# Agent attention with a maxout network: constant matmuls and the order of work at the end of the first stage

## Chip, core and metric

The kernel runs on one core of a Trainium2 chip. The metric is device time in microseconds (us) for one launch. Before the change the median of 5 runs is 474.26 us (473.52 to 474.63). The profile is one more execution of the same program.

## What is computed

The inputs have 4 batches of 12544 tokens with 128 channels, and 49 agents per batch. Attention goes from the agents to the tokens, then from the tokens to the agents, and a maxout network with three first layers follows:

```python
scale = 1.0 / np.sqrt(q.shape[-1])
def sm(a, b):
    s = scale * (a @ b.transpose(0, 2, 1))
    e = np.exp(s - s.max(-1, keepdims=True))
    return e / (e.sum(-1, keepdims=True) + 1e-09)
agent_v = sm(agents, k) @ v          # 4 x 49 x 128
x = (sm(q, agents) @ agent_v).reshape(B * S, D)
h = np.maximum(np.maximum(x @ w1, x @ w2), x @ w3)   # 768 wide
out = h @ w_out
```

For each batch, agent_v can be multiplied with the weights once. The kernel does so: "the product" of a batch is a table G of 49 rows that holds agent_v times the weights (and times differences of weights), and a query's exponentials are then multiplied with G directly.

## The kernel before

**First stage.** The product of batch 0 needs all keys and values of batch 0. They come in 12 groups, ten of 9 blocks of 128 tokens and two of 4 blocks (groups 10 and 11). One group goes through these steps (`k_group` with `early` set):

- SP issues the loads of keys and values (L218) into a pool of 14 buffers, `st`.
- GpSimd (POOL in the profile) casts the keys (L223), ScalarE (ACT) casts the values (L228).
- TensorE (PE) turns the keys, block by block, into PSUM (`turn_k`, L237), and VectorE (DVE) copies them out (`evacuate`, L243).
- TensorE computes the scores (L255), ACT the exponentials (L260).
- TensorE multiplies the exponentials with the values (L266) and with ones for their sums (L269), DVE adds both to an accumulator (L276).

These steps are staggered: the scores of a group stand behind the turning of the next group, its values behind the turning of the one after that.

**End of the first stage.** `k_tail` takes the reciprocal of the sums (L335) and multiplies (L338) into `avT`. `product` then runs ten matmuls in two halves (L350); ACT copies the first half out to G (L357), DVE the second (L355). Query group 0 is turned by TensorE (`turn_q`, L413), copied by DVE (L417), scored (L427), and ACT takes its exponentials (L433).

**Second stage.** There are 49 query groups. Each goes through hidden matmuls against G (L453), relu and maximum on ACT and DVE (L468, L465, L476, L478) and output matmuls (L483, L492). The first query groups also "host" one key group each of the next batch. Host key group 0 is turned on TensorE (L237). Later ones are turned by a DMA that SP issues (L239), so their scores (L255) wait for that DMA. GpSimd casts their keys (L223) and values (L230) and the queries (L408). In the first query groups there is no output work yet, and `ramp` puts constant matmuls (L575) where it would be.

**Constant matmuls.** `keep_busy` (L200) multiplies the identity with a constant tile of 128 x 512 into a PSUM tile that nobody reads. From group 4 on, the kernel places three of them after each group's turning and three after its scores and values; more stand among the steps of the end of the first stage.

**Order.** Every step is put into a list by `at(key, ...)`, with a key that is its place in time on an invented scale (6.0 units for a group), the names it needs, and the PSUM ring that it takes a tile from. `emit` sorts the list and issues the steps in that order, a step that lacks what it needs being put off until it can go. There are two rings: `uv`, three tiles of two banks, and `om`, two tiles of one bank. Each engine executes its own instructions in the order of issue. The tile framework adds the semaphore waits. `last_key` is the key of group 11, two units ahead of `KEY["u0"]`, the first hidden matmuls of query group 0.

Of the kernel before, what the change touches and what calls it, by code (L numbers as in the profile page):

```python
# [16 lines left out]
def kernel(  # L17
# [64 lines left out]
    def uv_tile(dtype=FP32):  # L82
        return psum.tile([P, 2, 512 if dtype == FP32 else 1024], dtype, tag="uv", bufs=3, name="uv_ps")
# [6 lines left out]
    def at(key, fn, name=None, needs=(), ring=None, frees=()):  # L90

        ops.append((key, len(ops), fn, name, needs, ring, frees))
# [55 lines left out]
    def load_tile():  # L150
        return loads.tile([P, KT, C], FP32, tag="st", name="st")
# [58 lines left out]
    def k_group(b, t0, n, key, s):  # L210

        d = {}
        early = s is None

        def load():
            for name, src in (("k", k), ("v", v)):
                t = d[name] = load_tile()
                nc.sync.dma_start(t[:, :n, :], src[b, t0 * P:(t0 + n) * P, :].rearrange(  # L218
                    "(p j) c -> p j c", j=n))

        def cast_k():
            d["kb"] = work.tile([P, KT, C], BF16, tag="k_bf", bufs=3, name="k_bf")
            nc.gpsimd.tensor_copy(out=d["kb"][:, :n, :], in_=d["k"][:, :n, :])  # L223

        def cast_v():
            d["vb"] = work.tile([P, KT, C], BF16, tag="v_bf", bufs=4, name="v_bf")
            if early:
                nc.scalar.activation(d["vb"][:, :n, :], d["v"][:, :n, :], AF.Copy)  # L228
            else:
                nc.gpsimd.tensor_copy(out=d["vb"][:, :n, :], in_=d["v"][:, :n, :])  # L230

        def turn_k():
            d["kT"] = work.tile([P, KT, P], BF16, tag="kT", bufs=3, name="kT")
            if early or s == 0:
                t = d["kT_ps"] = uv_tile(BF16).rearrange("p i c -> p (i c)")
                for j in range(n):
                    nc.tensor.transpose(t[:, j * P:(j + 1) * P], d["kb"][:, j, :], ident)  # L237
            else:
                nc.sync.dma_start_transpose(out=d["kT"][:, :n, :],  # L239
                                            in_=d["kb"][:, :n, :].rearrange("p j c -> p (j c)"))  # L240

        def evacuate():
            nc.vector.tensor_copy(out=d["kT"][:, :n, :].rearrange("p j c -> p (j c)"),  # L243
                                  in_=d["kT_ps"][:, :n * P])

        def scores():
            if early:
                d["pair"] = uv_tile()
                d["s"] = d["pair"][:, 0, :]
                last_tile["t"] = d["s"]  # L250
            else:
                d["s"] = host[s]
            t = d["s"]
            for j in range(n):
                nc.tensor.matmul(t[:, j * A:(j + 1) * A], d["kT"][:, j, :], agT[:, b, :A],  # L255
                                 start=(j == 0), stop=True, skip_group_check=True)

        def exps():
            d["e"] = work.tile([P, KT * A], BF16, tag="e_k", bufs=3, name="e_k")
            nc.scalar.activation(d["e"][:, :n * A], d["s"][:, :n * A], AF.Exp, scale=scale)  # L260

        def values():
            t, c = (d["pair"][:, 1, :], 0) if early else (d["s"], CV)
            for j in range(n):
                e = d["e"][:, j * A:(j + 1) * A]
                nc.tensor.matmul(t[:, c:c + A], d["vb"][:, j, :], e, start=(early and j == 0),  # L266
                                 stop=True, skip_group_check=True)
                if early:
                    nc.tensor.matmul(t[:, A:2 * A], ones_bf, e, start=False, stop=True,  # L269
                                     skip_group_check=True)  # L270

        def add_values():
            w = 2 * A if early else A
            src = d["pair"][:, 1, :w] if early else d["s"][:, CV:CV + A]
            if t0:
                nc.vector.tensor_tensor(out=Vacc[b], in0=src, in1=Vacc[b], op=ALU.add)  # L276
            else:
                Vacc[b] = work.tile([P, w], FP32, tag=f"Vacc{w}", name="Vacc")
                nc.vector.tensor_copy(out=Vacc[b], in_=src)

        def add_exps():
            if t0:
                nc.gpsimd.tensor_tensor(out=Eacc[b][:, :n * A], in0=Eacc[b][:, :n * A],  # L283
                                        in1=d["e"][:, :n * A], op=ALU.add)
            else:
                Eacc[b] = work.tile([P, KT * A], FP32, tag="Eacc", name="Eacc")
                nc.gpsimd.tensor_copy(out=Eacc[b], in_=d["e"])

        if early:
            g = ("early", t0)  # L290
            at(key - 30, load)
            at(key - 5, cast_k)
            at(key - 4, cast_v)
            at(key, turn_k, ("kt", g), (), "uv", [("kt_out", g)])
            at(key + 0.5, evacuate, ("kt_out", g), [("kt", g)])

            last = [("normalise", 0)] if t0 + n == NT else []
            at(min(key + 6.6, last_key + 0.6), scores, ("ks", g), [("kt_out", g)], "uv",
               [("ka", g)] + last)
            at(min(key + 7, last_key + 0.65), exps, ("ke", g), [("ks", g)])  # L300
            done = last_key + (0.55 if key < last_key - 6.5 else 0.8)
            at(min(key + 13.2, done), values, ("kv", g), [("ke", g)])
            at(min(key + 13.6, done + 0.01), add_values, ("ka", g), [("kv", g)])
        else:
            at(key + KEY["ks"] - 22, load)
            at(max(key + KEY["ks"] - 10, last_key - 3.4), cast_k)
            at(max(key + KEY["ks"] - 8, last_key - 3.3), cast_v)
            if s:
                at(max(key + KEY["ks"] - 6.5, last_key - 3.2), turn_k, ("kt_out", s))
            else:  # L310
                at(last_key + 0.87, turn_k, ("kt", s), (), "uv", [("kt_out", s)])
                at(last_key + 1.6, evacuate, ("kt_out", s), [("kt", s)])
            at(key + KEY["ks"], scores, ("ks", s), [("kt_out", s), ("ho", s)])
            at(key + KEY["ke"], exps, ("ke", s), [("ks", s)])
            at(key + KEY["ke"] + 1.5, add_exps, ("kx", s), [("ke", s)])
            at(key + KEY["kv"], values, ("kv", s), [("ke", s)])
            at(key + KEY["ka"], add_values, ("ka", s), [("kv", s)])
# [63 lines left out]
    def q_group(s):  # L381
        pairs = [range(0, 2), range(2, 4)]
        n, nh = GT, GT // 2
        parts = split(s * GT, (s + 1) * GT, 2)
        key = 6.0 * s
# [125 lines left out]
        def put(name, fn, *needs, ring=None, frees=()):  # L511
            at(key + K[name], fn, (name, s), needs, ring, frees)
# [3 lines left out]
        if s == 0:  # L516
            at(last_key - 29.9, load)
            at(last_key - 3.5, cast)
            at(last_key + 0.81, turn_q, ("qt", 0), (), "om", [("qe", 0)])
            at(last_key + 0.82, evacuate, ("qe", 0), [("qt", 0)])  # L520
            at(last_key + 1.2, scores, ("s", 0), [("qe", 0)], "om", [("ex", 0)])
            at(last_key + 1.21, exps, ("ex", 0), [("s", 0)])
        elif s < SB:
            at(key + K["qt"] - 20, load)
            at(max(key + K["qt"] - 7, last_key - 3), cast)
            put("qt", turn_q, ring="om", frees=[("qe", s)])
            put("qe", evacuate, ("qt", s), *([("s", s - 3)] if s >= 3 else []))
        else:
            at(key + K["s"] - 24, load)
            at(key + K["s"] - 8, cast)  # L530
            at(key + K["s"] - 5.5, turn_q_dma, ("qe", s))
# [47 lines left out]
    first_sizes = [KT] * (NT // KT) + ([NT % KT // 2, NT % KT - NT % KT // 2] if NT % KT else [])  # L579
    last_key = KEY["u0"] - 2  # L580
# [7 lines left out]
    fillers = []  # L588
    for g, n in enumerate(first_sizes):
        k_group(0, sum(first_sizes[:g]), n, first_key + 6.0 * g, None)  # L590

        if g >= 4:
            fillers += [(first_key + 6.0 * g + 0.55, 3), (first_key + 6.0 * g + 1.3, 3)]
    k_tail(0, last_key, (KEY["u0"] - 0.15, KEY["u0"] - 0.14), None)
    for key, n in fillers + [(last_key + 0.88, 3), (KEY["u0"] - 0.05, 4)]:
        at(key, lambda n=n: keep_busy(n), ("busy", key), (), "om", [("busy", key)])
    tails = {b * NT // GT: b for b in range(1, B)}
    hosting = set()
    for b in range(1, B):
        for g in range(NK):  # L600
            s = (b - 1) * NT // GT + g
# [5 lines left out]
    for s in range(NQ):  # L607
        q_group(s)
# [34 lines left out]
```

## Time and profile before

| what | us |
| --- | --- |
| median of 5 runs | 474.26 |
| lowest, highest | 473.52, 474.63 |
| profiled execution | 473.19 |
| its span, first to last instruction | 471.3 |
| TensorE busy in the span | 441.2 (94%) |
| DVE, ACT, POOL busy | 407.9, 395.8, 166.3 |
| turning of group 9 starts | 39.52 |
| last value matmul of the first stage starts | 46.69 |
| product starts | 49.49 |
| scores of host key group 0 start | 51.24 |

Times of events are us from the start of the span. The chain of work that ended last is found from the last instruction backwards: at each step to what released it, or to the instruction before it on its engine. In the timeline a row has the start, the duration, the engine, the line, the operation and its tiles; in square brackets stands how long the engine had been idle before and what ended that. PEld is TensorE's loading of weights, which overlaps its matmuls; SPq is SP issuing a DMA.

### The profile page before, as it was taken

To read this page: it belongs to the slowest core of one execution; us is meant where nothing else is said; L and a number is where in the kernel's file an instruction comes from. 1 tells how busy PE (TensorE), PEld (TensorE's weight loads), DVE (VectorE), ACT (ScalarE), POOL (GpSimd) and SP (SyncE) were. 2 spreads that over 40 slices of the span, in tenths; PEclk is the share of its full clock that TensorE was granted. 3 is DMA by queue.
4 is the path that set the end of the run, shared out by engine and by line. 5 is a ranking of instruction groups with operands and counts; after the bars stand their busy time and mean duration, and the time that the engine had idled before them with its cause. 6 is when DMAs were issued, how large, how long until landed. Compare 5 with 4: busy or idle time off the path is not lost.

```text
span 471.3 us, 13379 instructions
## 1 busy us (share of the span) xinstructions
PE 441.2 (94%) x5495; PEld 275.1 (58%) x5502; DVE 407.9 (87%) x519; ACT 395.8 (84%) x460; POOL 166.3 (35%) x166
## 2 busy tenths in 40 slices
PE   2489999999998999999999999999989999999996
PEld 2366456566664766666655766666655555555554
DVE  3153689999998999999998999999998999999995
ACT  3265798989888989889898899898989999999992
POOL 3244755363451463544360635445130011010000
PEclk9999999999999999999999999999999999999999
DMA  8999999997987999996988899985534757554412
GB/s 322 395 411 405 348 342 353 317 322 165 324 276 248 290 311 259 336 283 215 309 246 300 276 278 326 280 254 163 155 113 138 207 170 203 137 156 94 109 77 105
DMA packets 80649, 118.06 MB, mean 250 GB/s; under 512 B 54407, under 2 KB 55883, under 8 KB 80587
## 3 DMA queue, kind: packets, MB, share of 16 engines
q1 hardware_dynamic: 80384, 117.10, 80.0%
q8 instruction: 43, 0.70, 0.6%
q14 instruction: 19, 0.16, 0.1%
q10 hardware_dynamic: 203, 0.10, 0.1%
HBM read 78.74 MB, written 25.69 MB: 222 GB/s over the span
## 4 chain that ended last, share of the span: by engine, by line
PE 81%; DVE 8%; DMA 4%; ACT 4%; issue 2%; SPq 0%; POOL 0%; DVEq 0%; ACTq 0%; POOLq 0%
PE uv_ps L453 32%; PE o_ps L492 27%; PE o_ps L483 5%; DVE r L478 5%; DMA st<-in_k_dram 4%; PE m_ps L413 4%; PE m_ps L427 3%; PE m_ps L200 3%; ACT a_sb L468 3%; PE m_ps L255 1%; PE m_ps L266 1%; PE uv_ps L237 1%; DVE o_sb L499 1%; PE m_ps L441 1%; PE uv_ps L350 1%
## 5 line engine op out<-in xcount | busy, mean ns | idle before, releaser
L478 DVE TENSOR_TENSOR r<-uv_ps,a_sb 128x1024 bf16<-128x1024 f32 x245 | 297.5, 1221 | 15.7 <-PE uv_ps L453 6.1
L468 ACT ACTIVATE a_sb<-uv_ps 128x1024 bf16<-128x1024 f32 x245 | 241.2, 1027 | 10.9 <-PE uv_ps L453 10.5
L453 PE MATMUL uv_ps<-e_q,G 49*128 49x512 bf16 (+3 forms) x1248 | 185.5, 368 | 5.3 <-DVE r L478 3.1
L492 PE MATMUL o_ps<-wo_bf,r 128*128 128x128 bf16 x2352 | 176.4, 220 | 0.0
L492 PEld LDWEIGHTS <-r 128*128 128x128 bf16 x2352 | 137.7, 98 | 44.0 <-issue 42.6
L453 PEld LDWEIGHTS <-G 49*128 49x128 bf16 x1248 | 56.2, 93 | 66.3 <-issue 31.7
L283 POOL TENSOR_TENSOR Eacc<-Eacc,e_k 128x441 f32<-128x441 f32 (+1 forms) x30 | 30.5, 1016 | 131.7 <-ACT e_k L260 131.7
L499 DVE TENSOR_TENSOR o_sb<-o_ps,recips 128x512 f32<-128x512 f32 x98 | 67.6, 690 | 9.8 <-PE o_ps L492 7.1
L408 POOL CAST q_bf<-st 128x1024 bf16<-128x1024 f32 x49 | 51.1, 1042 | 69.7 <-DMA qT<-q_bf 67.9
L476 ACT ACTIVATE r<-uv_ps 128x1024 bf16<-128x1024 f32 x49 | 50.2, 1025 | 26.3 <-PE uv_ps L453 26.3
L223 POOL CAST k_bf<-st 128x1152 bf16<-128x1152 f32 (+2 forms) x45 | 50.7, 1127 | 31.4 <-DMA st<-in_k_dram 25.7
L465 ACT ACTIVATE uv_ps<-uv_ps 128x1024 f32<-128x1024 f32 x49 | 49.6, 1013 | 0.6 <-ACT a_sb L468 0.3
L483 PE MATMUL o_ps<-G,e_q 128*128 128x256 bf16 x196 | 38.0, 275 | 1.8 <-DVE o_sb L499 1.8
L230 POOL CAST v_bf<-st 128x1152 bf16<-128x1152 f32 (+1 forms) x33 | 37.5, 1136 | 0.3 <-DMA st<-in_v_dram 0.3
L433 ACT ACTIVATE e_q<-m_ps 128x512 bf16<-128x512 f32 x49 | 29.8, 609 | 2.4 <-PE m_ps L427 2.4
L483 PEld LDWEIGHTS <-e_q 128*128 128x128 bf16 x196 | 12.8, 97 | 20.6 <-issue 20.5
L228 ACT ACTIVATE v_bf<-st 128x1152 bf16<-128x1152 f32 (+1 forms) x12 | 12.8, 1071 | 13.9 <-DMA st<-in_v_dram 13.9
L417 DVE COPY qT<-m_ps 128x1024 bf16<-128x1024 bf16 x36 | 24.5, 681 | 0.0
L413 PEld LDWEIGHTS <-q_bf 128*128 128x128 bf16 x288 | 16.3, 97 | 13.8 <-issue 12.6
L243 DVE COPY kT<-uv_ps 128x1152 bf16<-128x1152 bf16 (+1 forms) x13 | 9.2, 705 | 16.9 <-PE uv_ps L237 16.9
L413 PE MATMUL m_ps<-ident,q_bf 128*128 128x128 bf16 x288 | 22.2, 220 | 0.0
L237 PE MATMUL uv_ps<-ident,k_bf 128*128 128x128 bf16 x107 | 10.5, 258 | 10.2 <-POOL k_bf L223 9.3
(67 smaller groups left out, 240.5 us busy)
## 6 DMA issues: line engine op xcount, KB each, us to landing
st<-in_q_dram SPq DMA_DIRECT2D x46, 512.0 KB, 4.4
out_dram<-o_sb SPq DMA_DIRECT2D x46, 512.0 KB, 3.3
st<-in_k_dram SPq DMA_DIRECT2D x40, 576.0 KB, 6.4
st<-in_v_dram SPq DMA_DIRECT2D x40, 576.0 KB, 7.2
st<-in_k_dram SPq DMA_DIRECT2D x3, 512.0 KB, 5.1
st<-in_v_dram SPq DMA_DIRECT2D x3, 512.0 KB, 6.9
wst<-in_moe_w_dram SPq DMA_DIRECT2D x3, 384.0 KB, 10.4
st<-in_q_dram SPq DMA_DIRECT2D x2, 384.0 KB, 3.9
```

The source lines that it names most:

```text
L223: nc.gpsimd.tensor_copy(out=d["kb"][:, :n, :], in_=d["k"][:, :n, :])
L230: nc.gpsimd.tensor_copy(out=d["vb"][:, :n, :], in_=d["v"][:, :n, :])
L408: nc.gpsimd.tensor_copy(out=d["qb"], in_=d["q"])
L413: nc.tensor.transpose(t[:, j * P:(j + 1) * P], d["qb"][:, j, :], ident)
L453: nc.tensor.matmul(t[:, h, j0 * P:j1 * P], G[b][h * H:h * H + A, col + f * P:col + (f + 1) * P], d["e"][h * H:h * H + A, j0 * P:j1 * P], s ...
L465: nc.scalar.activation(u, u, AF.Relu)
L468: nc.scalar.activation(a_sb[f], u, AF.Relu)
L476: nc.scalar.activation(r, v_ps[f], AF.Relu)
L478: nc.vector.tensor_tensor(out=r, in0=v_ps[f], in1=a_sb[f], op=ALU.max)
L483: nc.tensor.matmul(t[:, i * 2 * C:(i + 1) * 2 * C], d["e"][:, jj * P:(jj + 1) * P], G[batch[jj]][:, C1O:C1O + 2 * C], start=(i == 0), stop ...
L492: nc.tensor.matmul(t[:, c:c + C], r_sb[f][:, h, jj * P:(jj + 1) * P], wo_bf[:, f, :], start=False, stop=True, skip_group_check=True)
L499: nc.vector.tensor_tensor(out=d["out"][:, j:j + m, :], in0=d["o", o].rearrange("p (j c) -> p j c", c=C), in1=d["r"][:, j:j + m].unsqueeze( ...
```

## The change

Three things are done, all at the end of the first stage:

- The constant matmuls after the turning and after the values of groups 9, 10 and 11 go (18 in all), as do three ahead of the query scores and four behind the product. Six new ones stand in three pairs. In all there are 19 fewer.
- The scores, exponentials and values of groups 9, 10 and 11 get new keys, so that the values of group 9 stand ahead of the scores of group 10.
- The product of batch 0 stands ahead of the turning of query group 0 and of host key group 0. On TensorE the order becomes: first half of the product, turning of the query group, second half, two constant matmuls, query scores, turning of host key group 0, its scores. DVE takes the reciprocal ahead of the copy of the turned queries, and copies the second half of the product ahead of the turned keys. ACT copies the first half of the product ahead of the query exponentials.

```diff
-            at(min(key + 6.6, last_key + 0.6), scores, ("ks", g), [("kt_out", g)], "uv",
-               [("ka", g)] + last)
-            at(min(key + 7, last_key + 0.65), exps, ("ke", g), [("ks", g)])
-            done = last_key + (0.55 if key < last_key - 6.5 else 0.8)
+            late = max(0, (key - last_key) / 6 + 2)
+            at(min(key + 6.6, last_key + 0.58 + 0.02 * late), scores, ("ks", g), [("kt_out", g)],
+               "uv", [("ka", g)] + last)
+            at(min(key + 7, last_key + 0.64 + 0.01 * late), exps, ("ke", g), [("ks", g)])
+            done = last_key + (0.6 + 0.1 * late if late >= 1 else 0.55)
...
-                at(last_key + 0.87, turn_k, ("kt", s), (), "uv", [("kt_out", s)])
+                at(last_key + 1.3, turn_k, ("kt", s), (), "uv", [("kt_out", s)])
...
-            at(last_key + 0.81, turn_q, ("qt", 0), (), "om", [("qe", 0)])
-            at(last_key + 0.82, evacuate, ("qe", 0), [("qt", 0)])
+            at(last_key + 0.97, turn_q, ("qt", 0), (), "om", [("qe", 0)])
+            at(last_key + 0.98, evacuate, ("qe", 0), [("qt", 0)])
...
-        if g >= 4:
+        if 4 <= g < len(first_sizes) - 3:
             fillers += [(first_key + 6.0 * g + 0.55, 3), (first_key + 6.0 * g + 1.3, 3)]
-    k_tail(0, last_key, (KEY["u0"] - 0.15, KEY["u0"] - 0.14), None)
-    for key, n in fillers + [(last_key + 0.88, 3), (KEY["u0"] - 0.05, 4)]:
+    k_tail(0, last_key, (last_key + 0.95, last_key + 1.0), None)
+    for key, n in fillers + [(last_key + 0.61, 2), (last_key + 0.82, 2), (last_key + 1.1, 2)]:
```

## The prediction

> **What bounds the kernel now.** I read four views: the chain of work that ended last, the same chain in order of time, the timeline by engine, and the busy time by window.
>
> ```profile
> PE 81%; DVE 8%; DMA 4%; ACT 4%; issue 2%; SPq 0%; POOL 0%; DVEq 0%; ACTq 0%; POOLq 0%
> 10.93 11.02 DMA st<-in_k_dram
> 23.30 1.14 PE uv_ps L237 x9
> 39.03 0.65 PE m_ps L200 x3
> 39.68 0.50 PE uv_ps L237 x9
> 40.19 0.65 PE m_ps L200 x3
> 40.83 0.22 PE uv_ps L255 x9
> ...
> 47.87 0.59 PE m_ps L200 x2
> 48.80 0.75 PE m_ps L200 x3
> 49.56 0.88 PE uv_ps L350 x10
> 50.44 0.97 PE m_ps L200 x4
> 51.41 0.24 PE m_ps L255 x9
> ...
> 59.17 0.22 PE m_ps L255 x9
> ```
>
> Columns of the lower lines: start, us, what. The last wait for a load is at 22; from 23.3 TensorE's queue sets the time, and constant matmuls (L200, 0.216 us each, three in 0.65) lie in that chain. After the first stage TensorE is busy for 7.85 to 8.00 us of every 8, so a hand-over that is earlier moves the whole rest, unless a transfer is then late. Which transfer could be:
>
> ```profile
> 47.80 1.15 POOL L223 CAST k_bf<-st 128x1152 bf16<-128x1152 f32 x1 [1.54 <-DMA st<-in_k_dram]
> 48.98 1.35 SPq L239 DMA_TRANSPOSE kT<-k_bf  x1
> 58.49 1.15 POOL L223 CAST k_bf<-st 128x1152 bf16<-128x1152 f32 x1 [2.80 <-DMA kT<-k_bf]
> DMA to landing us min/median/max: 5.6/8.2/9.4
> 58.80 0.49 PEld L255 LDWEIGHTS <-kT 128*128 128x128 bf16 x9
> 45.00:50.00 5.00, 4.57 (x76) 3.04 (x76) 2.77 (x9) 1.16 (x3) 3.35 (x4) 1.00 1.03 413
> 50.00:55.00 5.00, 4.45 (x52) 2.15 (x48) 3.01 (x6) 4.29 (x5) 5.00 (x6) 1.00 1.08 399
> ```
>
> Three timeline rows, the landing times of the DMA transposes of 46 to 80 us, a timeline row, and two windows (last columns: granted clock, DMA share, GB/s). The keys of host step 1 were loaded by 47.80, cast by 48.95, given to the transposing DMA at 48.98, and landed 9.4 us later, at 58.4 (POOL's next cast waited for it until 58.49). TensorE loaded them as weights at 58.80, only 0.4 us later. All DMA engines are full throughout (share 1.03 to 1.08, about 400 GB/s), so this landing hangs on bytes queued ahead, not on TensorE.
>
> **The change part by part.** SP's 240 rows and POOL's 150 keep their order: no DMA is moved or added. TensorE's, DVE's and ACT's orders differ only up to the first hidden matmuls of query group 0. I worked the new order forward from the turning of group 9 (39.52 in both).
>
> *Fillers out, first part.* (Which copy a matmul waits for is read from the waits in the two built programs.) From 39.52 to the end of the last value matmuls (46.71) 15 constant matmuls go, 15 x 0.2165 = 3.25 us, and two come back ahead of the scores of group 11 (0.43). They hid latencies that now show. Turning group 10 waits for the copy of group 9 out of the same PSUM buffer (L243, 40.22 + 0.76 = 40.98), TensorE being free at 40.70: 0.35. Turning group 11 waits for the copy of group 10, 0.02. The values of group 9 wait for its exponentials, 0.14. The last two value groups wait for their exponentials 0.10 and 0.33 (0.58 together before). Waits rise by 0.36: last value matmul at 46.71 - 3.25 + 0.43 + 0.36 = 44.25, 2.45 earlier. Loads allow it: the casts of keys 10 and 11 ended at 39.60 and 40.92, and are now read at 41.05 and 41.98.
>
> *Hand-over.* Before, 46.71 to the scores of key group 0 at 51.24 took 4.53: query turning 0.45, key turning 0.50, fillers, scores 0.34, fillers, product 0.88, four fillers 0.87. DVE's query copy (0.69) stood ahead of the reciprocal. After: last sum add (L276, 0.26) ends at 44.74, reciprocal 0.46, multiply 0.21, avT at 45.41 (two fillers beside it, then TensorE idle 0.6). First half of the product 0.50, query turning 0.45, second half 0.38, two fillers 0.43, at 47.38 query scores 0.34, key turning 0.50, and the copy of the keys (0.75) now bare: scores at 49.24, which is 4.99. DVE's G copy (0.96, till 48.20), put ahead of that copy, ends 0.2 before it is wanted. ACT's G copy (till 47.14) and query exponential (till 48.48) are covered by the key turning and the 1.0 us that TensorE waits. This part costs about 0.45, and my rows give the old order 0.2 too short here, so compute gains 2.45 - 0.45 - 0.2 = **1.8 us** at the scores of key group 0. Bounds: 1.2 if each of six new hand-overs costs 0.1 more, 2.0 without the correction.
>
> *What is late next.* From 51.24 to 59.01 the order is the old one, so TensorE reaches the scores of host step 1 at 59.0 - 1.8 = 57.2. Their keys land at 58.4. Queued behind these scores on TensorE are all hidden matmuls of groups 0 and 1; ACT and DVE wait for those. So 1.3 of the 1.8 us become a wait, and **0.4 to 0.55 us** remain (58.80 to 58.4 by the weight load, 59.01 to 58.45 by the matmul); I take 0.5. From other rows: a landing in 5.6 us instead of 9.4 would be at 54.6, no cap, all 1.8; a landing 0.5 later leaves 0. I take 9.4, being this transfer's own. The next such transfer, issued at 55.32, lands at 63.5 by the median of 8.2, for scores at 67.65: covered. Later casts wait on compute, not on loads.
>
> So the profiled execution, 473.19 (span 471.3 and 1.9 around it), becomes 473.19 - 0.5 = **472.7**.
>
> *Against the median.* That execution is 1.07 below the median (474.26) and below all five runs (473.52 to 474.63). One cause is visible:
>
> ```profile
> 23.30 1.14 PE L237 MATMUL uv_ps<-ident,k_bf 128*128 128x128 bf16 x9 [5.90 <-POOL k_bf L223]
> 27.11 0.67 PE L237 MATMUL uv_ps<-ident,k_bf 128*128 128x128 bf16 x9
> 12.20:15.60 3.40, 2.70 (x41) 2.56 (x42) 1.02 (x2) 2.07 (x3) 1.15 (x1) 1.00 1.01 404
> 32.00:35.40 3.40, 2.06 (x28) 1.43 (x27) 2.37 (x5) 1.27 (x2) 1.35 (x2) 1.00 1.02 408
> ```
>
> Nine turnings took 1.14 us at 23.30 and 0.67 at 27.11, with a granted clock of 1.00 in each window: the column does not show it, the durations do. Matmuls ran at half pace until about 26. Were that moment later in other runs, all of TensorE's path to 59 would be later by half the delay, and the DMA landing at 58.4 would not. The new kernel reaches it 1.3 us early, so it would swallow a lateness of up to 1.3 and end near 472.7 all the same. That cause is not shown by one profile; if the 1.07 is spent elsewhere, the result is 474.26 - 0.5 = 473.7.
>
> [...] The rows: 2.06 busy of 3.4 us at 32.0 stayed at full pace, while 2.70 of 3.4 at 12.2 did not bring it on.
>
> **The rivals.**
> - *Cap holds, median's lateness swallowed*: 472.7 (472.2 to 473.3).
> - *Cap holds, lateness is elsewhere*: 473.7 (473.4 to 474.1), no change by 0.2% (0.95 us, about what a measurement can tell from no change). For it: nothing in the page shows run-to-run lateness at TensorE. Against: all five runs lie above the profiled one.
> - *No cap*, because the transposes land earlier or host step 1 has slack I do not see: 473.19 - 1.8 = 471.4, to 474.26 - 1.8 = 472.5 from the median. Against: full DMA engines.
> - *Nothing comes*: the keys land 0.5 later, or the third sum add and reciprocal wait on work I placed elsewhere: 474.3.
> - *Slower: the pace halves.* My walk leaves TensorE busy 2.4 of 3.4 us around 47 to 50, and 2.1 of 3.4 up to 58.4 with the wait for keys, as poor as the 2.06 that held. If it still drops at 47 and stays down until the dense stage at about 60, that is up to 6 us of work at double time; dropped for the 2.8 us that the warm-up took after 23.30, it costs 1.4. New time = 471.4 + loss, so 1.3 is free, beyond 3.8 us of loss it is slower by over 0.2%, and 6 gives 477.4; I take 477.
>
> **How the numbers follow.** Cap with lateness swallowed 0.45, cap alone 0.24, no cap 0.15, nothing 0.05, half pace 0.11. Faster by over 0.2% (under 473.3) is the first and third, 0.60; within 0.2% the second and fourth, 0.29; slower 0.11. The likeliest is 472.7. The range goes from 471.5 (most of the no-cap case) to 474.6 (nothing gained, with the runs' spread), and leaves out the half pace and a corner of no cap, some 0.16.
>
> **What would show it.** Right: no L200 between the turnings of groups 9 to 11; L276 for group 11 ending near 44.7; scores of key group 0 near 49.2; then TensorE idle about 1.3 us before the L255 matmuls of host step 1, released by the DMA transpose, at about 58.5; SP's issue of it still near 49.0; all later rows 0.5 earlier. Wrong: that transfer landing well before 58, half-pace matmuls (nine turnings in 1.14 us instead of 0.67) after 40, or key group 0's scores later than 50.5.

## The result, and the profile after

The changed kernel takes 472.97 us (median of 22 runs, 472.15 to 475.07). The kernel before, run beside it, takes 474.12 us (42 runs, 473.20 to 476.96). The ratio is 0.9977, with a 95% interval of 0.9968 to 0.9985: faster by 0.23%. The profiled execution took 472.44 us, with a span of 470.6.

The share of each engine in the chain that ended last, and four rows of that chain in order of time (start, us, what), both of the changed kernel:

```profile
PE 75%; DMA 12%; DVE 7%; ACT 3%; issue 2%; POOL 0%; SPq 0%; DVEq 0%; ACTq 0%; POOLq 0%
```

```profile
38.75 8.77 DMA st<-in_k_dram
...
47.63 1.15 POOL k_bf L223
48.78 0.03 POOL q_bf L409
48.81 9.39 DMA kT<-k_bf
58.20 0.05 issue
58.25 0.40 PE m_ps L255 x9
```

Before, the chain ran through TensorE's constant matmuls from 39 to 59 us. Now it runs through a load, GpSimd's cast and the transposing DMA of host step 1, and TensorE's share fell from 81% to 75% while the DMA's rose from 4% to 12%. The end of the first stage no longer sets the time in this execution: a transfer does.

The timeline of the changed kernel, at the places that the prediction named:

```profile
39.88 0.67 PE L237 MATMUL uv_ps<-ident,k_bf 128*128 128x128 bf16 x9
...
44.62 0.18 PE L269 MATMUL uv_ps<-e_k,ones_bf 128*128 128x49 bf16 x1
44.90 0.26 DVE L276 TENSOR_TENSOR Vacc<-uv_ps,Vacc 128x98 f32<-128x98 f32 x1 [0.26 <-PE uv_ps L269]
45.70 0.21 DVE L339 TENSOR_TENSOR avT<-Vacc,uv_ps 128x49 bf16<-128x49 f32 x1
45.97 0.62 PE L351 MATMUL uv_ps<-wall,avT 128*64 128x512 bf16 x6 [0.73 <-DVE avT L339]
48.81 1.35 SPq L239 DMA_TRANSPOSE kT<-k_bf  x1
49.92 0.40 PE L255 MATMUL m_ps<-agT,kT 128*128 128x49 bf16 x9 [0.85 <-DVE kT L243]
57.48 0.39 PE L576 MATMUL o_ps<-busy,ident 128*128 128x512 bf16 x1
58.25 0.40 PE L255 MATMUL m_ps<-agT,kT 128*128 128x49 bf16 x9 [0.38 <-DMA kT<-k_bf]
58.31 1.15 POOL L223 CAST k_bf<-st 128x1152 bf16<-128x1152 f32 x1 [2.78 <-DMA kT<-k_bf]
```

The turning of group 9 starts at 39.88, 0.36 later than before, ahead of everything that the change touches. From there to the scores of host key group 0 (L255 at 49.92) it takes 10.04 us, where it took 51.24 - 39.52 = 11.72 before: compute gained 1.68. From 49.92 the order is the old one, and TensorE would have been at the scores of host step 1 at 57.70 (the constant matmul at 57.48 and 0.22 more). It started them at 58.25, released by the DMA of `kT`, as was GpSimd's cast. Before, they started at 59.01, without a wait:

```profile
59.01 0.39 PE L255 MATMUL m_ps<-agT,kT 128*128 128x49 bf16 x9
```

The gain there is 0.76, and it stays: the copies of the outputs (`o_sb`) lie 0.76 to 0.79 earlier from 65 us to the last one at 466.

The two windows shown of before (4.57 and 4.45 us of TensorE's time then) read now:

```profile
45.00:50.00 5.00, 3.42 (x36) 1.65 (x35) 3.19 (x7) 1.62 (x2) 3.49 (x4) 1.00 1.03 409
50.00:55.00 5.00, 4.22 (x48) 2.04 (x49) 3.24 (x5) 4.04 (x5) 5.00 (x6) 1.00 1.07 405
```

TensorE is idle for 1.6 of 5 us, the clock stayed up in this execution, and the DMA engines are as full as before.

### The profile page after: what moved, and what is told of

It reads as the page before. It is cut to its first block, busy times and chain, and to the rows that moved or that the text cites. A ratio compares the mean times of both kernels' runs of the same rounds, so it can differ in the third digit from the quotient of the medians.

```text
span 470.6 us, 13342 instructions
## 1 busy us (share of the span) xinstructions
PE 439.0 (93%) x5477; PEld 273.5 (58%) x5483; DVE 408.1 (87%) x519; ACT 396.0 (84%) x460; POOL 166.0 (35%) x166
## 4 chain that ended last, share of the span: by engine, by line
PE 75%; DMA 12%; DVE 7%; ACT 3%; issue 2%; POOL 0%; SPq 0%; DVEq 0%; ACTq 0%; POOLq 0%
PE uv_ps L454 31%; PE o_ps L493 28%; DMA st<-in_k_dram 7%; PE o_ps L484 5%; DVE r L479 5%; PE m_ps L414 3%; PE m_ps L428 3%; DMA wst<-in_moe_w_dram 2%; DMA kT<-k_bf 2%; ACT a_sb L469 2%; PE m_ps L255 1%; PE m_ps L266 1%; DMA ag_st<-in_agents_dram 1%; DVE o_sb L500 1%; PE m_ps L442 1%
## 5 line engine op out<-in xcount | busy, mean ns | idle before, releaser
L260 ACT ACTIVATE e_k<-m_ps 128x441 bf16<-128x441 f32 (+1 forms) x33 | 19.1, 578 | 1.5 <-PE m_ps L255 1.5
```

## Experiments

The granted clock given with an execution is its mean over it. Two of the profiles below hold a fall in the middle of the run: the clock is 0.50 from 51.92 to 55.34 in one and from 59.34 to 62.75 in the other. One such window of 3.41 us takes 3.41 x 0.5 / 471 = 0.0036 off the mean, so 0.996 and less is read as at least one in the middle of the run, an estimate. In the profile of before the clock is also 0.50 from 469.87, behind the last matmul, to the end at 471.3; that takes 0.0015 off its mean, which is 0.998.

**The change again.** The changed kernel itself, for a second profile.

> The changed kernel as it is, beside the others on the same chip. Cap theory (the landing of host step 1's turned keys, not TensorE, sets the hand-over): about 473.0 us, with TensorE idle 0.5 to 1.3 us ahead of the scores of host step 1 and their weight load within 0.1 us of the landing of the DMA transpose near 58.2. Rival (the shorter path is all there is, the wait is incidental): the same time, but runs that differ by as much as those of the kernel before.

Measured: 472.83 us (9 runs, 472.46 to 474.87), ratio 0.9977 (0.9965 to 0.9989). The runs lie 2.4 us apart, those of the kernel before beside them 1.8, so the cap does not draw them together. The profiled execution was a late one, 474.49 us:

```profile
28.22 1.17 PE L237 MATMUL uv_ps<-ident,k_bf 128*128 128x128 bf16 x9
...
42.31 0.67 PE L237 MATMUL uv_ps<-ident,k_bf 128*128 128x128 bf16 x9
...
58.82 1.15 POOL L223 CAST k_bf<-st 128x1152 bf16<-128x1152 f32 x1 [2.68 <-DMA kT<-k_bf]
60.13 0.39 PE L255 MATMUL m_ps<-agT,kT 128*128 128x49 bf16 x9
```

The nine turnings at 28.22 are still at half pace. The trace's record of the granted clock has full pace from 29.47, against 27.32 in the first profile of this kernel and 26.14 in that of before. The turning of group 9 came at 42.31 and not at 39.88, and the keys (landed at 58.7) had been there for 1.4 us when TensorE came for them at 60.13. So the same program is bound by the transfer in one execution and by TensorE in another. That the moment of full pace makes the difference is tried further below.

**The load behind the transpose.** From 48.8 to 58.2 the DMA engines of the changed kernel have a share of 1.09 (352 GB/s), and two loads were issued just ahead of the transpose (L218 at 44.89 and 46.15). In the changed kernel the keys and values of host step 3 are loaded later, behind that transpose:

```diff
-            at(key + KEY["ks"] - 22, load)
+            at(key + KEY["ks"] - (18 if s == 3 else 22), load)
```

> The changed kernel with the loads of host step 3's keys and values (1.18 MB) issued behind the DMA transpose of host step 1 instead of ahead of it; nothing else moves. Cap theory: 1.18 MB at 0.41 MB per us is 2.9 us less ahead of the transpose, it lands near 55.5, TensorE goes on without a wait at about 57.7 instead of 58.25, and the time falls by 0.5 us (by up to 0.7) to about 472.4. Rival: nothing hung on the landing, no change (473.0).

The changed kernel with this edit, timeline:

```profile
48.87 2.38 SPq L239 DMA_TRANSPOSE kT<-k_bf  x1
49.10 0.40 PE L255 MATMUL m_ps<-agT,kT 128*128 128x49 bf16 x9 [0.85 <-DVE kT L243]
56.88 0.39 PE L255 MATMUL m_ps<-agT,kT 128*128 128x49 bf16 x9
```

Issued at 48.87, the transpose landed at 55.4, 2.8 us earlier than without the edit, and the scores of host step 1 started without a wait: 17.83 us after the turning of group 9 (39.05), against 18.37 in the changed kernel and 19.49 before. Every later row lies 2.11 us ahead of before. The times missed the expected 472.4: 472.93 us (12 runs, 471.21 to 474.81), ratio 0.9971 (0.9957 to 0.9984), against 472.83 without the edit. In the profiled execution 1.2 us of the gain were gone between the last output copy and the end. The trace shows that the cap was this transfer and went; the median doesn't resolve what that is worth here.

**The same load edit in the kernel before.**

> The kernel before with the same move of two loads. Cap theory: there TensorE came 0.4 us after the landing, so the earlier landing gains nothing: 474.1, no change within 0.2 us, with the transpose landing near 55.5. Rival (the order of loads helps by itself, whatever TensorE does): 0.5 us faster as in the changed kernel.

Measured: 473.88 us (12 runs, 473.20 to 475.17), ratio 0.9998 (0.9988 to 1.0008). The transpose landed at about 55.5, and the scores of host step 1 stood at 59.03, as without the edit (59.01). The transfer bounds nothing until TensorE is earlier.

**Constant matmuls alone.** The change has two halves: 18 constant matmuls of groups 9 to 11 out, and a new order. The first half in the kernel before:

```diff
-        if g >= 4:
+        if 4 <= g < len(first_sizes) - 3:
```

> The kernel before with nothing but the 18 constant matmuls of groups 9, 10 and 11 taken out (the order of the product, the query turning and the rest as before). From the start of group 9's turning to the scores of host key group 0 it took 11.7 us before and 10.0 in the changed kernel. My walk by the same rows gives 8.6 to 8.8 here, so taking matmuls out alone shortens the path more than the whole change. Cap theory: the time is that of the changed kernel all the same (472.6 to 473.0), and the wait ahead of the scores of host step 1 is longer by 1.2. Rival (the new order brings part of the gain): scores later than 10.0, time between 473.0 and 474.2.

Measured: 474.09 us (12 runs, 472.71 to 476.07), ratio 0.9998 (0.9983 to 1.0013). The expectation missed. Its profile, from the fastest of the 12:

```profile
39.52 0.67 PE L237 MATMUL uv_ps<-ident,k_bf 128*128 128x128 bf16 x9
...
48.09 0.39 PE L255 MATMUL m_ps<-agT,kT 128*128 128x49 bf16 x9
...
55.63 0.39 PE L575 MATMUL o_ps<-busy,ident 128*128 128x512 bf16 x1
58.38 0.40 PE L255 MATMUL m_ps<-agT,kT 128*128 128x49 bf16 x9 [2.36 <-DMA kT<-k_bf]
```

The path came out as expected: 48.09 - 39.52 = 8.57 us, 3.15 less than before, and then a wait of 2.36 us for the same transfer. The four executions with a mean clock of 0.998 or more took 472.71, 472.86, 472.94 and 473.67 us. The other eight had 0.990 to 0.996 and took 473.78 to 476.07. TensorE loses pace in two of three executions.

**The order alone.** The changed kernel with those 18 constant matmuls put back.

```diff
-        if 4 <= g < len(first_sizes) - 3:
+        if g >= 4:
```

> The changed kernel with the 18 constant matmuls of groups 9, 10 and 11 put back: the new order alone. My walk gives 13.1 to 13.3 us from the turning of group 9 to the scores of host key group 0, 1.4 to 1.6 later than before: 475.7, slower by 0.3%. Rival (the new order brings part of the gain): 11.7 us or less, 474.2 or faster.

```profile
40.70 0.67 PE L237 MATMUL uv_ps<-ident,k_bf 128*128 128x128 bf16 x9
...
54.12 0.40 PE L255 MATMUL m_ps<-agT,kT 128*128 128x49 bf16 x9 [0.85 <-DVE kT L243]
61.89 0.39 PE L255 MATMUL m_ps<-agT,kT 128*128 128x49 bf16 x9
```

Measured: 476.20 us (6 runs, 475.91 to 478.07), ratio 1.0047 (1.0030 to 1.0064), 0.5 above what was expected. The scores of host key group 0 stand 13.42 us after the turning of group 9, 1.70 later than before, and no transfer hides it (61.89 - 54.12 = 7.77, no wait). So the two halves have opposite signs: the constant matmuls out give 3.15 us of path, the order costs 1.70 with them in and 10.04 - 8.57 = 1.47 with them out.

**Constant matmuls alone, with the load edit.** The kernel of the fillers alone, and the load of host step 3 behind the transpose.

> Fillers alone, and the loads of host step 3 behind the transpose of host step 1, which then lands near 55.5. Cap theory: the whole 2.9 us of the shorter path comes through, 474.2 - 2.9 = 471.3, with no wait ahead of the scores of host step 1, and runs that differ by as much as those of the kernel before. Rival (no cap, or a later bound): 472.5 to 473.0 as without the move of loads.

Measured: 471.57 us (7 runs, 470.49 to 474.03), ratio 0.9949 (0.9930 to 0.9967). The scores of host step 1 start at 56.51 without a wait, later rows lie 2.47 to 2.50 ahead of before, and one execution of 7 (474.03, clock 0.994) shows lost pace, not 8 of 12. The path's gain came back, and with the wait for the keys nearly all of the lost pace went; the one execution that still lost it was not profiled.

**One group more.** The changed kernel without the six constant matmuls of group 8 too.

```diff
-        if 4 <= g < len(first_sizes) - 3:
+        if 4 <= g < len(first_sizes) - 4:
```

> The changed kernel with group 8's six constant matmuls taken out as well (1.30 us of TensorE; some 0.4 of it comes back as waits for copies, so the path ends 0.9 earlier). Cap theory: the wait ahead of the scores of host step 1 grows by that 0.9, the time stays at 472.7 to 473.0. Rival without a cap: 0.9 us faster, 472.1. Clock rival: matmuls at half pace appear after 40 us and the time rises by 1 us or more.

Measured: 473.01 us (8 runs, 472.48 to 473.52), ratio 0.9974 (0.9965 to 0.9984): nothing gained on the changed kernel, with the scores of host step 1 at 58.48 and their keys landed at 58.43, as the cap has it. Five of 8 had a clock of 0.994, and the profile holds such a window (start and end, length, busy time of PE, PEld, DVE, ACT and POOL, then granted clock, DMA share, GB/s):

```profile
48.51:51.92 3.41, 2.29 (x38) 1.31 (x35) 1.27 (x5) 2.09 (x4) 3.41 (x4) 1.00 1.03 410
51.92:55.34 3.42, 3.14 (x17) 1.29 (x17) 2.78 (x3) 2.24 (x3) 3.42 (x5) 0.50 1.30 388
```

The clock was 0.50 for 3.42 us. The window ahead of it, busy for 2.29, holds the new hand-over: the turning of host key group 0, 0.85 us idle for the copy of its keys, its scores, the first hidden matmuls. The time lost came out of the wait for the keys, so it cost little. No wait for a transfer lies in that window: its longest idle, the 0.85 us, belongs to the new order itself.

**A bridge over the wait.** The kernel of the fillers alone loses pace in two of three executions, by the wait for the keys or by the gaps that the missing matmuls leave. Nine constant matmuls go onto TensorE just ahead of the scores of host step 1, where it waits anyway:

```diff
                 at(key - 6, fill, ("filled", o) if i == NF - 1 else None, [("fill", o)])
+        for _ in range(9):
+            at(6.0 + KEY["ks"] - 0.01, fill, None, [("fill", 0)])
```

> The kernel before without the 18 constant matmuls of groups 9 to 11, as in the run with the fillers alone out, and with nine constant matmuls more on TensorE just ahead of the scores of host step 1, where that run's profile shows it idle for 2.36 us, waiting for the turned keys. They take 9 x 0.2165 = 1.95 us and fit into the wait. Theory that the wait lets TensorE's pace drop (in the run with the fillers alone, 8 of 12 executions had a mean granted clock of 0.996 or less, and the four others 472.7 to 473.7): the drops go, every execution has a mean clock of 0.998 or more, the median falls from 474.1 to 472.8, between 472.6 and 473.1, and the slowest stays under 474. Rival, the drops come from the gaps that the missing matmuls leave between 40 and 48: as many executions drop as before, median 474 to 474.3.

```profile
55.85 2.33 PE L577 MATMUL o_ps<-busy,ident 128*128 128x512 bf16 x10
58.03 0.40 PE L255 MATMUL m_ps<-agT,kT 128*128 128x49 bf16 x9
...
58.80 0.82 PE L453 MATMUL uv_ps<-e_q,G 49*128 49x512 bf16 x6
```

Measured: 473.00 us (12 runs, 472.11 to 473.91), ratio 0.9978 (0.9969 to 0.9987). All 12 have a clock of 0.997 or more, where 0.998 was expected, so by the measure above none lost a window, and the median is 1.1 us below that without the bridge. The wait was the cause in this kernel. The run with the load edit, which kept its pace in six of 7 executions, is 1.4 us faster still (471.57): with the pace kept in both, that is what the transfer holds back.

**The same, caught in a profile.** The kernel of the fillers alone once more, for a second profile.

> The kernel of the run with the fillers alone out once more, for a second profile. If an execution over 473.7 is profiled, the clock's record should show one or two windows of 3.41 us at half pace: after the wait for the keys of host step 1 (from about 57 to 61), if the wait is the cause; between 44 and 50, if the gaps left by the missing matmuls are. An execution at 472.7 to 473 shows none.

It took 474.52 us, and the trace's clock record falls to half at 59.34 and returns at 62.75. Two windows and the timeline around them:

```profile
55.93:59.34 3.41, 1.59 (x16) 0.56 (x16) 2.18 (x2) 1.93 (x4) 0.62 (x2) 1.00 0.91 242
59.34:62.75 3.41, 3.41 (x21) 1.12 (x20) 1.23 (x1) 2.36 (x3) 3.41 (x4) 0.50 1.02 383
```

```profile
56.71 0.39 PE L575 MATMUL o_ps<-busy,ident 128*128 128x512 bf16 x1
58.78 0.40 PE L255 MATMUL m_ps<-agT,kT 128*128 128x49 bf16 x9 [1.69 <-DMA kT<-k_bf]
...
59.70 1.46 PE L453 MATMUL uv_ps<-e_q,G 49*128 49x512 bf16 x6
```

The wait of 1.69 us lies whole in the window 55.93 to 59.34, and the next window runs at half pace: six hidden matmuls take 1.46 us, where they take 0.82 in the run with the bridge, and three constant matmuls at 61.09 take 1.46, where they take 0.82 there. In the first profile of the same program the wait was longer, 2.36 us from 56.02 to 58.38, and the clock held at 1.00, with TensorE busy for 1.93 in the window that has most of it:

```profile
56.90:60.31 3.41, 1.93 (x19) 0.76 (x20) 0.79 (x2) 1.06 (x2) 1.86 (x2) 1.00 1.02 357
```

**Full pace early, kernel before.** TensorE is idle from 17.4 to 23.3. Sixteen constant matmuls there bring full pace earlier, in the kernel before:

```diff
-    for key, n in fillers + [(last_key + 0.88, 3), (KEY["u0"] - 0.05, 4)]:
+    for key, n in fillers + [(first_key + 23.9, 16), (last_key + 0.88, 3), (KEY["u0"] - 0.05, 4)]:
```

> The kernel before with 16 constant matmuls added in TensorE's idle time ahead of 23.3 us, so that full pace comes at about 20.5 in each execution, as in the run that had them (20.47), and not between 25.9 and 29.5. The turning of group 9 then starts at 38.4 to 38.6, TensorE would reach the scores of host step 1 at 58.0, and the cap is the landing of their keys at 58.4. Theory that the lateness of the median comes from the moment of full pace: the median falls from 474.1 to 472.7 (472.5 to 473.0), the executions lie within 1 us, and the changed kernel's gain is all but had without its change. Rival, the lateness is elsewhere: at most the 0.5 us up to the cap, 473.6 to 474.1, with the old spread of 2 us.

```profile
17.46 4.35 PE L200 MATMUL m_ps<-busy,ident 128*128 128x512 bf16 x16
23.49 0.68 PE L237 MATMUL uv_ps<-ident,k_bf 128*128 128x128 bf16 x9 [1.68 <-POOL k_bf L223]
...
58.67 0.40 PE L255 MATMUL m_ps<-agT,kT 128*128 128x49 bf16 x9 [0.31 <-DMA kT<-k_bf]
```

Measured: 472.47 us (6 runs, 472.24 to 472.72), ratio 0.9967 (0.9955 to 0.9979). Full pace came at 18.96 by the clock record, the nine turnings at 23.49 take 0.68 and not 1.14, and TensorE meets the keys of host step 1 as they land. The runs' spread went from 2.1 us (23 runs beside it, 473.00 to 475.12) to 0.5. In the profile of before and the two of the changed kernel, which are alike up to group 9, full pace came at 26.14, 27.32 and 29.47 us and the turning of group 9 at 39.52, 39.88 and 42.31. So most of the lateness that the prediction could only conjecture is the moment of full pace. Not all of the smaller spread is: in the profile TensorE now reaches the cap 0.31 us early, which hides lateness up to that. The median is 0.5 us below that of the changed kernel, though the two intervals overlap.

**Full pace early, changed kernel.** The same 16 constant matmuls.

> The changed kernel with the same 16 constant matmuls. TensorE would reach the scores of host step 1 at about 56.4 and must wait 2 us for their keys at 58.4. By the cap, the median is that of the kernel before with these matmuls, within 0.3: 472.4 to 472.8, against 472.9 without them. Without a cap it would be 471.2. If a wait of 2 us for keys is what lets the pace drop, several executions have a mean clock of 0.996 or less and are 0.5 to 3 us longer, and the median is 472.6 to 473.8.

```profile
58.20 0.40 PE L255 MATMUL m_ps<-agT,kT 128*128 128x49 bf16 x9 [1.88 <-DMA kT<-k_bf]
```

Measured: 473.96 us (12 runs, 472.27 to 475.64), ratio 0.9994 (0.9979 to 1.0010). The three executions at 0.999 took 472.27, 472.45 and 472.73, which is the kernel before with these matmuls to 0.1 us: by the cap the change is then worth nothing. The nine others had clocks of 0.990 to 0.996, and the median is 1.5 us above that of the same edit on the kernel before. The change, with TensorE early, makes a wait of 1.9 us. That the wait makes the pace drop, as with the fillers alone, is likely here and not shown: none of the nine was profiled, and the hand-over of the new order can lose the pace too. For the wait speaks the cost: a window lost ahead of the wait would be paid out of it, as in the run with one group more, and eight of the nine took 473.71 us or more.

**All three.** Constant matmuls of groups 9 to 11 out, load of host step 3 behind the transpose, and the 16 early ones, in the old order.

> As the one above, with 16 constant matmuls on TensorE while it waits for group 4's keys (17.4 to 23.3 us), so that full pace comes before 24 us in every run and not somewhere between 25.8 and 29.5. If the lateness of runs comes from that moment: the median falls to the fastest runs of the one above, about 470.4 (473.2 - 2.9 + 0.1), runs within 0.6 us of each other; the turning of host key group 0 stays at 44.9, where its cast ends, so no more than that. Rival (lateness is from elsewhere): same median and spread as the one above.

```profile
65.71 0.40 PE L255 MATMUL m_ps<-agT,kT 128*128 128x49 bf16 x9 [1.04 <-DMA kT<-k_bf]
```

Measured: 471.17 us (6 runs, 470.29 to 472.00), ratio 0.9935 (0.9919 to 0.9951), 0.8 above what was expected, and the runs lie 1.7 us apart where 0.6 was expected: with full pace early, some spread of another cause, not found here, is left. The scores of host step 1 came at 55.86 without a wait; those of host step 2 then waited for their own keys until 65.71, and the lead over before fell from 3.15 to 1.9 us. The cap moved on to the next transfer. It beats both kernels, with the lowest median of these programs; its interval and that of the run without the early matmuls overlap.

Executions that lost at least one window of pace, by the mean clock, beside the wait for the keys of host step 1 in the profile:

| kernel | wait, us | lost pace |
| --- | --- | --- |
| before (beside the experiments) | 0 | 0 of 71 |
| before, load edit | 0 | 0 of 12 |
| changed (result; again) | 0.38; 0 | 1 of 22; 1 of 9 |
| changed, load edit | 0 | 1 of 12 |
| changed, one group more | 0 (pace lost before) | 5 of 8 |
| order alone | 0 | 1 of 6 |
| fillers alone (two profiles) | 2.36; 1.69 | 8 of 12; 1 of 1 |
| fillers alone, bridge | bridged | 0 of 12 |
| fillers alone, load edit | 0 | 1 of 7 |
| before, early pace | 0.31 | 0 of 6 |
| changed, early pace | 1.88 | 9 of 12 |
| all three | 0 (1.04 for host step 2) | 0 of 6 |

Most losses stand beside a long wait. The run with one group more shows that such a wait is not needed: there the pace fell ahead of it, behind the hand-over.

## Why the prediction was right, and where it was off

The time, 472.97, lies 0.3 from the 472.7 forecast and on the side that was given 0.60.

*Fillers out, first part: right.* The last value matmul was to be 2.45 us earlier. It started at 44.62, 4.74 after the turning of group 9; before, 46.69 - 39.52 = 7.17. The difference is 2.43.

*Hand-over: right to 0.1.* With the correction it was to lose 0.65 (0.45 and 0.2). It took 49.92 - 44.62 = 5.30 against 51.24 - 46.69 = 4.55 before, a loss of 0.75. So compute gained 1.68 where 1.8 was given, inside the bounds of 1.2 and 2.0. The terms that it lists from `avT` to the scores of key group 0 come to 0.5 less than its starts (45.41 and 1.76 is 47.17, not 47.38; 47.38 and 1.59 is 48.97, not 49.24), so that much latency stood in it without a name. What the step missed is that the two halves of the change have opposite signs, as it priced them only together: the order costs about 1.5 us of path, and the constant matmuls out give 3.15.

*Cap: right in mechanism, wrong in the size of the wait, 0.2 short in what remained.* The keys of host step 1 were to land at 58.4 and leave 0.4 to 0.55; they landed at 58.20 and left 0.76. The wait was put at 1.3 us and was 58.25 - 57.70 = 0.55. Of the 0.7 between, 0.36 is the later turning of group 9 in that execution, 0.2 the earlier landing, and 0.12 the smaller gain. The load edit shows that it was this transfer: the wait goes in the changed kernel, and in the kernel before nothing happens. The prediction's reading that TensorE is busy for 7.85 us or more of every 8 after the first stage leaves out some windows (6.44 at 139 to 147 us), but the gain came through them whole.

*Lateness swallowed: the cause right, the swallowing less than half.* The prediction said that other runs come to full pace later and that the slack would swallow up to 1.3 us of it. The early constant matmuls bear out the cause for most of the spread. But the median of the changed kernel stands 0.53 above its profiled execution (472.97 and 472.44), where before it stood 0.93 above (474.12 and 473.19): 0.40 of 0.93 was swallowed, not all. Two sizes were off. "Half the delay" is too little for late moments: from full pace at 26.14 (before) to 29.47 (second profile of the changed kernel), the turning of group 9 moved by 2.79, 0.8 of it; from 26.14 to 27.32, by 0.36, 0.3 of it. And the slack was nearer 0.55 than 1.3. An execution that comes later than that, such as the one at 474.49, is not capped and only keeps the 1.68. So the median gained 474.12 - 472.97 = 1.15, between the cap's 0.76 and the full 1.68, and not the 1.56 forecast. There is luck in the 0.3: the profiled execution came 0.26 below the 472.7 that was forecast for it, and lateness put the median 0.53 above that; the two errors have opposite signs.

*No cap* was refuted for early executions and is what late ones do. *Nothing comes* and *cap alone* (473.7) are refuted by the interval.

*Half pace: it does occur, the evidence was poor and the length wrong.* The changed kernel lost pace in 1 of 22 executions (475.07, clock 0.993), so its chance was not too small for this change. That 2.06 busy of 3.4 us at 32.0 stayed at full pace tells little: elsewhere the pace fell after 2.29 and 1.59 busy of 3.41 and held after 1.93. A drop lasted 3.41 us where a profile holds it, and some two times that, an estimate, by the lowest mean clocks (0.990, at 0.0036 each and with the end of the run in it); executions that lost pace took up to 3.5 us more than the fastest of their kernel (474.03 and 470.49), not the 6 that were priced. It decided the median in two kernels, fillers alone (by the wait, as the bridge shows) and the change with early pace (where the place is not shown). By these counts the costly new order does one useful thing: its 1.47 us come out of the wait that the removal alone leaves, and the changed kernel seldom loses the pace, though its own hand-over is a gap as well. So it has the lower median, 472.97 against 474.09 for the removal alone, though its path to the cap is longer.

## What to carry to other kernels

Before taking filler work out of a path, find the transfer that the path will reach next: here the gain ended there, and in the wait that appeared TensorE could lose its pace (8 of 12 executions, 0 of 12 with the wait bridged). Bridge such a wait with filler, or move loads behind the transfer that it waits for. Where the runs of one kernel spread by 2 us, look for the moment when the half-pace start ends, and bring it forward with work in an idle stretch; here that gave at least as much as the whole change (472.47 and 472.97).

## What the runs showed that was not expected

- The moment of full pace was 27.32 us in one profile of the changed kernel and 29.47 in another, and 26.14 in that of before. The two falls in the middle of a run that a profile holds lasted 3.42 and 3.41 us. At the end of the profile of before the clock fell 443.7 us after its rise (469.87 and 26.14).
- The clock column of a window shows 1.00 before the first rise too (22.73 to 26.14 in the profile of before), while nine turnings there, at 23.30, took 1.14 us and not 0.67. The durations tell it, the column doesn't.
- Busy time alone does not sort these windows. Pace fell after 2.29 and 1.59 us busy of 3.41, and held after 1.93 and, in the changed kernel with early pace, after 1.86 (56.65 to 60.06). What the clock goes by is not shown.
- A transposing DMA took 9.4 us from issue to landing behind queued loads and about 6.5 with one step's loads moved behind it.
